# A fused attention, Fourier-mix and MLP kernel: loads in a new order, and batch 1 by the way of the later batches

## The chip, the cores and the metric

The kernel runs on one core of one Trainium2 chip. The metric is device time of one execution in microseconds, the median of several runs. The engines are TensorE (PE; its weight loads are listed as PEld), VectorE (DVE), ScalarE (ACT), GpSimd (POOL) and SyncE (SP, which here only issues DMAs).

## The reference, cut to what matters

Two layers in a row, over 4 batches of 768 positions, 8 heads of 64 (512 features).

```python
# attention: q, k, v are (4, 8, 768, 64)
scores = q @ k.T / 8
keep   = (pos_k < 8) | ((0 <= pos_q - pos_k) & (pos_q - pos_k < 96))
dist   = where(pos_k < 8 and not local, 96, abs(pos_q - pos_k))
scores = where(keep, scores - slope[h] * dist, -1e9)
x      = softmax(scores) @ v            # heads side by side: (4, 768, 512)

# Fourier mix and MLP
u   = x + real(fft(fft(x, axis=positions), axis=features))
un  = (u - mean(u)) / sqrt(var(u) + 1e-6)
out = u + relu(un @ w_ch1) @ w_ch2      # w_ch1 (512, 2048), w_ch2 (2048, 512)
```

## The kernel before, in words

**The order of the work.** The program is written out by a planner (class `Plan`, lines 18 to 153) that runs once, when the kernel is built. It keeps a clock for every engine and for the DMA queues, with a cost for each step. Four lists of TensorE work wait in it: `MIX` (Fourier and normalisation), `ATT` (attention), `PH` and `PG` (the two MLP products). At each step it emits what can start first by its clocks; between equals an earlier list goes first. Work of the other engines, and each DMA issue, is queued with `pl.later` and goes to the engine that would end it first. What comes out is a fixed order on each engine; a semaphore wait stands wherever data or a buffer must be ready. SP and POOL issue their DMAs in that fixed order too, and a wait on one of them holds all that is behind it.

**Attention of one batch.** Heads go in four pairs. `load` brings q, k and v of a pair (384 KB each); `cast_qk` or `cast_direct` turns q and k to 16 bits; `trans` transposes them (twelve 128x128 products on PE and a copy `qkT` by DVE, L515 and L521, or, for batches 2 and 3, four DMA transposes, `trans_dma`, L494); `kg_copies` takes the 8 global keys out on POOL. `score` makes a pair's banded scores in three units. `glob`, `v_global` handle the global keys. `av` multiplies by v and its `norm` (L699, L700) writes the batch's x. Two ways exist:

- Batches 0 and 1: v is cast by POOL (`cast_v0`) and put in place by PE (`v_place`, L427, copies L443 and L444). The bias is added on PE by products of a diagonal `sid` with the distances `dist` (L542, L547), and ACT's exponential (L575) writes `ex` directly.
- Batches 2 and 3: v comes by a strided DMA (L336) and is cast in place (`cast_v`, L454). The exponential goes to `er` (L572) and DVE multiplies it by a table `mk` (L587). ACT makes `mk` with eight exponentials (L1128).

**Fourier mix of one batch.** `bounce` writes x to DRAM (`xd`) and reads it back with rows in another order (`xr`), on ACT's queue. `fold_3` (batch 0) or `fold_s` and `fold_d` add and subtract on DVE; `y_unit` (py, L881) is the transform over positions with tables `t1` and, in batch 0, `t1x`; `mirror` makes reversed copies on POOL (L916 to L918, L929); `u_unit` (pu, L961) is the transform over features, and its `add` (L980, L984) makes u and its mean; `un`, `nt_unit` (ptu, L1025) normalise and transpose.

**MLP.** A chunk is 256 rows; there are three in a batch. `ph_unit` (ph, L1053) makes 8 units of 8 products for a chunk, `pg_unit` (pg, L1076) 8 units of 4, and L1085 adds the result to u, which L1090 stores. Three chunks of `hT` fit.

**Loads and PSUM.** SP issues batch 0's loads, then batch 1's; q and k of batch 1 are staged in the buffers that later hold w1 and w2. POOL issues w1 and w2 (four parts each, fp32 in DRAM, cast by the DMA) when the casts of batch 1 have left those buffers (`wload`, L1164, L1169). SP then waits for the last part of w2 (`hold`, L1178) before the loads of batch 2. Four PSUM banks serve attention of batches 0 and 1 as rings `C` and `D`; when the last of these uses is over (token `("CD",)`) they become the banks of ph and pg.

```python
1180:         for b in range(B):
1181:             if b:
1182:                 for hp in range(HP):
1183:                     load(b, hp, "qk")
1184:                     load(b, hp, "v")
```

Of the kernel before, what the change touches and what calls it, by code (L numbers as in the profile page):

```python
# [14 lines left out]
P = 128  # L15


class Plan:
# [10 lines left out]
    def __init__(self):  # L29
        self.t = {"PE": 0.0, "ACT": 0.0, "DVE": 0.0, "POOL": 0.0, "SP": 0.7, "DMA": 1.9, "DMA2": 0.0}  # L30
        self.tok = {}
        self.ready = []
        self.pending = []
        self.rings = {}
        self.left = {}
        self.n = 0
# [49 lines left out]
    def emit(self, place):  # L86
# [6 lines left out]
        if dma:  # L93
            q = "DMA2" if eng == "ACT" or outs and outs[0][0] in ("xw", "xr") else "DMA"
            end = self.t[q] = max(self.t[q], end) + dma
        else:
            lat += self.LAT.get(eng, 0.0)
# [79 lines left out]
def kernel(  # L177
# [23 lines left out]
    FB = 2  # L201
    DB = 1
    assert (B, H, S, Dh, NG, NL) == (4, 8, 768, 64, 8, 96)
# [66 lines left out]
    def bank(tag, name, dtype=FP32):  # L270
# [4 lines left out]
        if "late" not in early:  # L275
# [6 lines left out]
            "ww": 1, "rev0": 1, "u": 4, "un": 2, "unT": 2, "w1": 1, "w2": 1}  # L282
# [21 lines left out]
    one = kon.tile([P, 1], FP16, tag="one", name="one")  # L304
    expst = [kon.tile([P, 2, 1408], FP16, tag=f"ex{hp}", name=f"ex{hp}") for hp in range(HP)]
# [13 lines left out]

    def load(b, hp, which):  # L320
        n = HP * b + hp
        h0 = 2 * hp
        gate = [("gate",)] if n == FB * HP else []
        if b >= FB:
            srcs = [(0, q), (1, k)] if which == "qk" else [(2, v)]
            for w, src in srcs:
                i = 2 + 3 * (n - FB * HP) + w

                def run(src=src, i=i, w=w):
                    t = stage[("t", n, w)] = buf("qs", i, [P, 2 * NS, Dh], FP32, 1)  # L330
# [6 lines left out]
                pl.later([("SP", 0.55 if w < 2 else 1.1, run)], free("qs", i) + gate, 0.0, [("ld", n, w)], lat=1.7, dma=2.67)  # L337
                if w < 2:
                    cast_direct(b, hp, w, i)
# [5 lines left out]
        else:  # L345
            tag, ti, users, slot = (("hT", hp, 2, 0) if hp < 3 else ("qs", 0, 1, None)) if b == 0 else \
                (("w1", "w2")[hp // 2], 0, 4, 2 * (hp % 2))
            for w, src in enumerate((q, k)):
                at = (tag, ti) if slot is not None else (tag, w)

                def run(w=w, src=src, at=at):
                    if slot is None:
                        t = buf(at[0], at[1], [P, NS, 2 * Dh], FP32, 1)
                    else:
                        if at not in stage:
                            stage[at] = buf(at[0], at[1], [P, users, NS, 2 * Dh], FP32, users)
                        t = stage[at][:, slot + w]
                    stage[("t", n, w)] = t
                    run_dma(t, src, b, h0)
# [15 lines left out]
    def cast_qk(b, hp, w, at):  # L375
# [9 lines left out]
        if b == 0 and not (w and hp):  # L385
            ways.append(("DVE", dve2(768), lambda: cast("DVE")))
        elif b == 0:
            ways = [("POOL", 0.87, lambda: cast("POOL"))]
        else:
            ways.append(("POOL", 0.87, lambda: cast("POOL")))  # L390
        pl.later(ways, [("ld", n, w)] + free("qk", n), 0.0, [("qk", n, w)], [("free",) + at], rank=b)

    def cast_direct(b, hp, w, i):
        n = HP * b + hp

        def cast(on):
            if n not in qk16:
                qk16[n] = buf("qk", n, [P, 2, 2, NP, 2, Dh], FP16, 1)
            for t in range(2):
                copy_on(on, qk16[n][:, t, w], stage[("t", n, w)].rearrange("p (h i t) d -> p t i h d", h=2, t=2)[:, t])  # L400
        pl.later([("ACT", act(768), lambda: cast("ACT")), ("POOL", 1.6, lambda: cast("POOL"))],
                 [("ld", n, w)] + free("qk", n), 0.0, [("qk", n, w)], [("free", "qs", i)], rank=1)
# [46 lines left out]
    def cast_v(b, hp):  # L449
        n = HP * b + hp  # L450
        i = 2 + 3 * (n - FB * HP) + 2
# [4 lines left out]
        pl.later([("POOL", 0.87, run)], [("ld", n, 2), ("avdone", b - 2)], 0.0, [("v", b, hp)], [("free", "qs", i)], rank=1)  # L456
# [6 lines left out]
    def BANKS(b):  # L463
        return ("xx", "C", "D") if b < 2 else ("xx",)

    def CD(b, ring):
        if b == 1 and ring in ("C", "D"):
            pl.left[("CD",)][0] += 1
            return [("CD",)]
# [4 lines left out]


# [27 lines left out]
    def trans(b, hp):  # L503
        if b >= FB:
# [3 lines left out]
        def run(start, ring):  # L508
            pt = bank("xx", f"pt_{n}", FP16)
            src = qk16.pop(n)  # L510
            for w in range(2):
                o = pt[:, w, 0:S].rearrange("p (n a t m) -> p n t a m", n=NP, a=2, t=2)
                for x in range(NP):
                    for t in range(2):
                        nc.tensor.transpose(o[:, x, t], src[:, w, x, t].rearrange("p h d -> p (h d)"), idn)  # L515
# [3 lines left out]
            def evac():  # L519
                TT[n] = buf("qkT", n, [P, 2, S], FP16, 6)  # L520
                V.tensor_copy(TT[n], pt[:, :, 0:S])  # L521

            def evac_act():
                TT[n] = buf("qkT", n, [P, 2, S], FP16, 6)
                A(TT[n], pt[:, :, 0:S], AF.Copy)
            pl.later([("DVE", dve2(2 * S), evac)] + [("ACT", act(2 * S), evac_act)] * (b < 2), free("qkT", n), e, [("qkT", n)], ring=ring, rank=RA(b))
            kg_copies(b, hp)
        ATT.append(([("qk", n, 0), ("qk", n, 1)], ("xx",), run))

    def score(b, hp, g):  # L530
        n = HP * b + hp
        idx = 2 * HP + 3 * (n - 2 * HP) + g

        def run(start, ring):
            pa = bank(ring, f"sc_{n}_{g}")
            w0, w1_ = ((256, CO), (CO, CO), (256, P))[g]
            tiles = ((2 * g, 0, w0), (2 * g + 1, 256, w1_))
            if b < 2:
# [10 lines left out]
            for i, c0, cw in tiles:  # L549
                for s in range(2):  # L550
                    lo = 64 * s
                    nc.tensor.matmul(pa[:, s, c0:c0 + cw], TT[n][lo:lo + 64, 1, i * P:(i + 1) * P],  # L552
                                     TT[n][lo:lo + 64, 0, i * P:i * P + cw], start=(b > 1), stop=True,
                                     skip_group_check=(b < 2))
            e = pl.pe(0.24 if b > 1 else 0.66, start)
# [17 lines left out]
            if b < 2:  # L573
                def direct():
                    A(cut(expst[hp][:, :, g * 512:g * 512 + (384 if g == 2 else 512)]), cut(pa), AF.Exp, 0.0, 0.125)  # L575
                pl.later([("ACT", act(2 * w), direct)], [("avh", 0, hp)] * b, e, [("ex", b, hp, g)], CD(b, ring), ring=ring, rank=RA(b))
# [3 lines left out]
            def mul():  # L580
# [4 lines left out]
                else:  # L585
# [3 lines left out]
                     [("er", idx), ("mk", hp)] + ([("avh", b - 1, hp)] if b else []), 0.0,  # L589
                     [("ex", b, hp, g)], [("free", "er", idx)], rank=RA(b))  # L590
        ATT.append(([("qkT", n)] + ([("sid", hp), ("c", "dist")] if b < 2 else []), BANKS(b), run))
# [58 lines left out]
    XT = [("x", 0), ("hT", 4), ("x", 1), ("x", 2)]  # L650
# [58 lines left out]
    def bounce(b):  # L709

        on, eng = "ACT", nc.scalar
# [16 lines left out]
        pl.later([(on, 0.5, rd)], [("xw", b, n) for n in range(len(parts))] + free("xr", b), 0.0, [("xr", b)], lat=1.7, dma=3.8 if b else 2.4)  # L728
# [53 lines left out]
    def IW(b, n):  # L782

        return 2 * b + n if b < DB else 3 * b - DB + n

    def fold_3(b):
# [17 lines left out]
        def g1():  # L804
            z = T[("z", b)]
            eg = T[("eg", b)] = buf("eA", IA(b, 0), [P, 2, 6, 256], FP16, 1)
            ww = T[("ww", b)] = buf("ww", IW(b, 0), [P, 20, P], FP16, 1)
# [20 lines left out]
    T1X = {}  # L828

    def fold_d(b, needs):  # L830
# [3 lines left out]
        def g1():  # L834
            z = T[("z", b)][:, 0:6]
            eg = T[("eg", b)] = buf("eA", ia, [P, 2, 6, 256], FP16, 1)
            ww = T[("ww", b)] = buf("ww", IW(b, NA(b)), [P, 20, P], FP16, 1)
# [29 lines left out]
    def y_unit(b, g):  # L867
        def run(start, ring):
# [17 lines left out]
            if g == len(YG) - 1:  # L886
                pl.used(("free", "eA", IA(b, NA(b))), e)
                pl.used(("free", "ww", IW(b, NA(b))), e)
            nb = (len(ys) + 1) // 2

            def cp(on, lo, hi):
                if ("y", b) not in T:
                    T[("y", b)] = buf("zy", 2 * b + 1, [P, 8, 2, 2, P], FP16, 7)
# [5 lines left out]
                for t in range(lo, hi):  # L899
                    for a in range(2):  # L900
                        Y[(b,) + ys[2 * t + a]] = T[("y", b)][:, 2 * g + t, a]
            cuts = [(0, nb)] if b else [(t, t + 1) for t in range(nb)]
            for x, (lo, hi) in enumerate(cuts):
                w = 512 * (hi - lo)
                pl.later([("ACT", act(w), lambda lo=lo, hi=hi: cp("ACT", lo, hi)),
                          ("DVE", dve(w), lambda lo=lo, hi=hi: cp("DVE", lo, hi))],
                         free("zy", 2 * b + 1), e, [("y", b) + y for y in ys[2 * lo:2 * hi]],
                         (CD(b, ring) if x == len(cuts) - 1 else []), ring=ring if x == len(cuts) - 1 else None)
        MIX.append(([("w", b, 0 if g in (0, 3) else 1)] + [("c", "t1")] + [("c", "t1x")] * (b < DB), BANKS(b), run))

    def mirror(b):

        def r0():
# [375 lines left out]
```

## Time and profile before

| | |
|---|---|
| median of 3 runs | 278.57 us (278.4 to 279.12) |
| profiled execution | 280.46 us, of which the span of the trace is 278.7 |
| granted TensorE clock | 0.999 |
| busy, share of span | PE 93%, PEld 62%, DVE 57%, ACT 53%, POOL 22% |
| PE products | 2448, in 258.7 us |
| HBM read, written | 31.92 MB, 9.44 MB |
| chain that ended last | PE 81%, DVE 8%, ACT 4% |

In the page, the busy tenths are the span in 40 slices of about 7 us. A row of the timeline is start, length, engine, source line, operation, output and inputs, and how many instructions were merged into it; lengths of products overlap, so a rate is read from the starts. "us to landing" of a DMA is from issue to the last byte.

### The profile page before, as it was taken

What the parts mean: (1) busy time and instruction counts of PE and PEld (TensorE: products, weight loads), DVE (VectorE), ACT (ScalarE), POOL (GpSimd) and SP (SyncE); (2) the same over time, 40 slices, a digit from 0 to 9 for tenths busy, and PEclk for the clock granted to TensorE, in tenths of its full rate; (3) what the DMA queues carried; (4) which work ended last, traced back from release to release, by engine and by line L of the source; (5) the groups of instructions that cost most, each with busy time, mean ns of one, the idle gap of its engine ahead of it and who ended that gap; (6) DMA issues with size and microseconds to landing.
All of it is one profiled execution on the core that took longest, in us unless ns stands there. A gap on an engine that the chain in (4) does not pass through costs nothing.

```text
span 278.7 us, 6005 instructions
## 1 busy us (share of the span) xinstructions
PE 258.7 (93%) x2448; PEld 173.2 (62%) x2448; DVE 157.9 (57%) x323; ACT 148.0 (53%) x255; POOL 60.8 (22%) x127
## 2 busy tenths in 40 slices
PE   1999789598789999999999999999999999999994
PEld 1445538458657874677486466777866677767441
DVE  4347781985786414766278968666896661111121
ACT  1466675495666642797782237889242256434000
POOL 1435365931002512412110021401001320100000
PEclk9999999999999999999999999999999999999999
DMA  7999999997774498978858895200164020110122
GB/s 206 290 291 257 339 304 196 207 204 119 194 204 144 105 167 162 231 137 165 196 146 196 214 263 104 66 2 0 40 136 168 1 78 1 40 38 22 56 75 75
DMA packets 70301, 40.69 MB, mean 146 GB/s; under 512 B 27394, under 2 KB 66306, under 8 KB 70274
## 3 DMA queue, kind: packets, MB, share of 16 engines
q1 hardware_dynamic: 61474, 29.83, 43.6%
q0 software_dynamic: 4224, 4.19, 9.3%
q10 hardware_dynamic: 4576, 6.29, 8.3%
q8 instruction: 19, 0.31, 0.5%
q14 instruction: 8, 0.07, 0.1%
HBM read 31.92 MB, written 9.44 MB: 148 GB/s over the span
## 4 chain that ended last, share of the span: by engine, by line
PE 81%; DVE 8%; ACT 4%; issue 2%; DMA 2%; POOL 1%; ACTq 1%; SPq 0%; DVEq 0%; POOLq 0%
PE pg L1076 29%; PE ph L1053 29%; PE py L881 5%; PE sc L552 4%; PE pav L680 3%; PE pu L961 3%; ACT ex L575 2%; PE pt L515 2%; DVE qkT L521 2%; PE ptu L1025 2%; DMA ident<-idm 2%; PE sc L547 2%; PE pav L669 1%; PE sc L542 1%; DVE sm L984 1%
## 5 line engine op out<-in xcount | busy, mean ns | idle before, releaser
L1053 PE MATMUL ph<-unT,w 128*128 128x256 f16 x768 | 93.8, 273 | 2.2 <-DVE hT L1060 2.2
L1076 PE MATMUL pg<-w,hT 128*128 128x512 f16 x384 | 89.9, 379 | 0.0
L1053 PEld LDWEIGHTS <-w 128*128 128x128 f16 x768 | 72.7, 98 | 18.4 <-issue 6.1
L1059 ACT ACTIVATE hT<-ph 128x512 f16<-128x512 f32 x73 | 43.6, 597 | 48.1 <-PE ph L1053 46.9
L1076 PEld LDWEIGHTS <-hT 128*128 128x128 f16 x384 | 36.8, 98 | 36.3 <-issue 0.4
L1085 DVE SCALAR_TENSOR_TENSOR u<-pg,sm,u 128x512 f32<-128x512 f32 x24 | 18.0, 750 | 53.7 <-PE pg L1076 53.5
L575 ACT ACTIVATE ex<-sc 128x992 f16<-128x992 f32 (+2 forms) x24 | 21.3, 925 | 15.1 <-PE sc L552 11.1
L1060 DVE TENSOR_SCALAR hT<-ph 128x512 f16<-128x512 f32 x23 | 15.9, 690 | 11.5 <-PE ph L1053 11.5
L572 ACT ACTIVATE er<-sc 128x992 f16<-128x992 f32 (+2 forms) x24 | 21.5, 923 | 1.6 <-PE sc L552 1.6
L1011 POOL TENSOR_SCALAR sm<-sm 128x2 f32<-128x2 f32 x12 | 3.2, 264 | 71.9 <-ACT un L1004 71.7
L929 POOL COPY ww<-zy 128x512 f16<-128x512 f16 x16 | 9.4, 613 | 42.4 <-PE py L881 42.4
L980 DVE SCALAR_TENSOR_TENSOR u<-pu,xr 128x512 f32<-128x512 f32 x24 | 15.6, 688 | 4.7 <-PE pu L961 4.0
L552 PE MATMUL sc<-qkT 64*128 64x256 f16 (+1 forms) x192 | 17.8, 275 | 0.2 <-DVE qkT L521 0.2
L369 ACT ACTIVATE qk<-qs 128x384 f16<-128x384 f32 (+1 forms) x31 | 14.5, 528 | 6.1 <-DMA qkT<-qk 4.8
L587 DVE TENSOR_TENSOR ex<-er,mk 128x992 f16<-128x992 f16 (+2 forms) x24 | 15.2, 645 | 3.8 <-ACT er L572 3.6
L995 ACT ACTIVATE un<-u,sm 128x512 f16<-128x512 f32 x12 | 8.5, 716 | 16.1 <-DVE sm L984 13.0
L680 PE MATMUL pav<-v,ex 128*128 128x65 f16 x352 | 16.4, 193 | 0.4 <-ACT ex L575 0.4
L680 PEld LDWEIGHTS <-ex 128*128 128x128 f16 x352 | 15.1, 97 | 1.8 <-issue 1.1
L552 PEld LDWEIGHTS <-qkT 64*128 64x128 f16 x192 | 6.0, 96 | 16.1 <-issue 13.2
L896 ACT ACTIVATE zy<-py 128x512 f16<-128x512 f32 (+1 forms) x10 | 8.1, 810 | 14.7 <-PE py L881 14.7
L1004 ACT ACTIVATE un<-un 128x512 f16<-128x512 f16 x24 | 14.8, 620 | 1.5 <-PE ptu L1025 1.4
L898 DVE CAST zy<-py 128x512 f16<-128x512 f32 (+1 forms) x9 | 8.3, 927 | 10.5 <-ACT zy L896 6.4
(101 smaller groups left out, 305.8 us busy)
## 6 DMA issues: line engine op xcount, KB each, us to landing
out_dram<-u SPq DMA_DIRECT2D x24, 256.0 KB, 2.2
w<-in_moe_w_ch_dram POOLq DMA_DIRECT2D x8, 512.0 KB, 11.8
qs<-in_q_dram SPq DMA_DIRECT2D x9, 384.0 KB, 4.7
qs<-in_k_dram SPq DMA_DIRECT2D x9, 384.0 KB, 5.4
u<-in_v_dram SPq DMA_DIRECT2D x8, 384.0 KB, 7.7
xr<-xd ACTq DMA_DIRECT2D x4, 768.0 KB, 4.3
qs<-in_v_dram SPq DMA_DIRECT2D x16, 192.0 KB, 3.9
w<-in_q_dram SPq DMA_DIRECT2D x4, 384.0 KB, 7.5
```

Source lines behind the costliest of these rows:

```text
L552: nc.tensor.matmul(pa[:, s, c0:c0 + cw], TT[n][lo:lo + 64, 1, i * P:(i + 1) * P], TT[n][lo:lo + 64, 0, i * P:i * P + cw], start=(b > 1), s ...
L572: A(mine(), cut(pa), AF.Exp, 0.0, 0.125)
L575: A(cut(expst[hp][:, :, g * 512:g * 512 + (384 if g == 2 else 512)]), cut(pa), AF.Exp, 0.0, 0.125)
L587: VT(o, mine(), m, op=ALU.mult)
L680: nc.tensor.matmul(po[:, jj, hh * 65:(hh + 1) * 65], lhsT, v16[b % 2][:, i, h, 0:65], start=(jp == 0 and a == 0), stop=(a == len(ops) - 1) ...
L980: V.scalar_tensor_tensor(u[:, a].rearrange("p (n r) -> p n r", r=4), pu[:, a].rearrange("p (r n) -> p n r", r=4), 1.0, XR[b][:, rr].rearra ...
L1004: A(x, x, AF.Square, accum_out=MV[c][:, a, 2:3])
L1053: nc.tensor.matmul(ph[:, a * CH:(a + 1) * CH], W1[0][:, d, jb * P:(jb + 1) * P], UNT[c][:, d, :], start=(d == 0), stop=(d == ND - 1))
L1059: pl.later([("ACT", act(512), lambda: A(dst, ph, AF.Relu)), ("DVE", dve(512), lambda: V.tensor_scalar_max(dst, ph, 0.0))], [], e, [("h", c ...
L1060: ("DVE", dve(512), lambda: V.tensor_scalar_max(dst, ph, 0.0))],
L1076: nc.tensor.matmul(pg, HT[c][:, jb, t * P:(t + 1) * P], W2[0][:, jb, :], start=(jb == 0), stop=(jb == NJ - 1))
L1085: V.scalar_tensor_tensor(UT[c][:, t, :], pg, MV[c][:, t, 3:4], UT[c][:, t, :], op0=ALU.mult, op1=ALU.add)
```

## The change

- **Batch 1** goes by the way of the later batches (`FB` from 2 to 1): v by the strided DMA, no `v_place`, no bias products, `er` and the product with `mk`. Its q and k are still transposed on PE (`PT`). `mk` is therefore made at the start (`MKA`). Only batch 0 uses the rings `C` and `D`.
- **Loads.** After batch 0: the tables `t1`, `t2`, q and k of pairs 0 and 1 of batch 1 (`EARLY`, into w2's buffer), `t1x`. w1 has a buffer free from the start and is issued when batch 0's last k is cast (`W1AT`). Batch 0's bounce is issued by SP. w2 is held by a two-element POOL copy (`seen`) until the bounce's read has landed. The rest of batch 1 is issued after that read (token `("xi",)`) into the three `qs` buffers. Batch 2 waits for part 2 of w2 (`WG`). The planner's costs of these DMAs are lowered.
- **Products of zeros.** Twelve 512-column products of the zeroed tile `EG` stand first on PE.
- **Small copies.** The global keys of a pair transposed on PE are copied from PSUM by the engine that copies `qkT` (`kg_now`). The reversed copies of `mirror`'s first part, and all of batch 0's, are made from PSUM by ACT or DVE (`back`, `turn`); batch 0's go to space behind `t1x`. In batch 0 ACT makes the mean instead of DVE.

```diff
-    FB = 2
+    FB = 1
     DB = 1
+    WG = 2
+    MKA = 4
+    EARLY = [(4, 0), (4, 1), (5, 0), (5, 1)]
+    W1AT = ("qk", 3, 1)
+    PT = (0, 1, 2, 3)
...
+    order = [(n, w) for n in range(HP, B * HP) for w in range(3) if n >= HP + 2 or w == 2]
+    def place(n, w):
+        return ("qs", 2 + order.index((n, w))) if (n, w) in order else ("w2", 0)
...
-                pl.later([("SP", 0.55 if w < 2 else 1.1, run)], free("qs", i) + gate, 0.0, [("ld", n, w)], lat=1.7, dma=2.67)
+                pl.later([("SP", 0.55 if w < 2 else 1.1, run)], free(*at) + gate + [("xi",)] * (b == 1 and (n, w) not in EARLY), 0.0, [("ld", n, w)], lat=1.7, dma=1.47 if w < 2 else 2.3)
...
     def BANKS(b):
-        return ("xx", "C", "D") if b < 2 else ("xx",)
+        return ("xx", "C", "D") if b == 0 else ("xx",)
...
+    def kg_now(b, hp, on, pt):
+        for s in range(2):
+            c0 = 16 * (hp % 2) + 8 * s
+            d = kG[b % 2][64 * s:64 * s + 64, hp, c0:c0 + NG].rearrange("p (t m) -> p t m", t=2)
+            x = pt[64 * s:64 * s + 64, 1, 0:P].rearrange("p (t m) -> p t m", t=2)[:, :, 0:NG // 2]
+            copy_on(on, d, x)
...
-            if b < 2:
+            if b == 0:
                 for s in range(2):
                     lhsT = sid[:, 2 * hp + s, :]
...
-        on, eng = "ACT", nc.scalar
+        on, eng = ("ACT", nc.scalar) if b else ("SP", nc.sync)
...
+            def back(on):
+                d = T[("y", b)][:, 7]
+                s0 = py[:, 0, :].rearrange("p (a c m) -> p a c m", a=2, c=2)
+                copy_on(on, d[:, 0, :, 0:1], s0[:, 0, :, 0:1])
+                copy_on(on, d[:, 0, :, 1:P], s0[:, 0, :, P - 1:0:-1])
+                copy_on(on, d[:, 1], s0[:, 1, :, ::-1])
+            def turn(on, t):
+                d = REV[0][:, 2 * g + t]
+                copy_on(on, d.rearrange("p a c m -> p (a c) m"), py[:, t, :].rearrange("p (x m) -> p x m", m=P)[:, :, ::-1])
...
-                V.tensor_scalar_mul(sm[:, :, 1], sm[:, :, 0], -SC / Dm)
+                if b:
+                    V.tensor_scalar_mul(sm[:, :, 1], sm[:, :, 0], -SC / Dm)
+                else:
+                    A(sm[:, :, 1], sm[:, :, 0], AF.Copy, 0.0, -SC / Dm)
...
+        V.memset(EG, 0.0)
+        pz = bank("xx", "pz")
+        for _ in range(12):
+            nc.tensor.matmul(pz[:, 0, :], EG[:, 0:P], EG, start=True, stop=True)
...
+                    nc.gpsimd.tensor_copy(seen, XR[0][0:1, 0, 0:2])
                     W2[0] = buf("w2", 1, [P, NJ, Dm], FP16, 1)
...
-            needs = [("vc", 5), ("free", "w1", 0)] if i == 0 else [("wl", 3), ("free", "w2", 0)] if i == 4 else [("wl", i - 1)]
+            needs = [W1AT] if i == 0 else [("wl", 3), ("free", "w2", 0), ("xr", 0)] if i == 4 else [("wl", i - 1)]
...
-            nc.sync.dma_start(g, W2[0][0:1, NJ - 1, 0:2])
-        pl.later([("SP", 0.45, hold)], [("w2", 3)], 0.0, [("gate",)])
+            nc.sync.dma_start(g, W2[0][0:1, 4 * WG, 0:2])
+        pl.later([("SP", 0.45, hold)], [("w2", WG)], 0.0, [("gate",)])
```

## The prediction

> **What bounds the kernel now.** I read the page's busy row first, then busy time by window, then the chain of waits in order of time, then the timeline around the places the chain names.
>
> ```profile
> PE 258.7 (93%) x2448; PEld 173.2 (62%) x2448; DVE 157.9 (57%) x323; ACT 148.0 (53%) x255; POOL 60.8 (22%) x127
> ...
> PE   1999789598789999999999999999999999999994
> ```
>
> TensorE is the bound, and all that it loses it loses early. Busy time by window says how much (columns: length, then PE busy and its instructions, and the other engines):
>
> ```profile
> 6.20:64.30 58.10, 50.91 (x633) 30.04 (x634) 38.30 (x87) 37.56 (x57) 30.20 (x51) 1.00 1.13 260
> 64.30:100.00 35.70, 33.08 (x339) 26.89 (x336) 21.12 (x40) 22.00 (x41) 6.33 (x11) 1.00 0.62 152
> 100.00:274.80 174.80, 174.67 (x1484) 116.29 (x1481) 95.47 (x186) 87.16 (x157) 23.26 (x56) 1.00 0.45 107
> ```
>
> From 100 us on PE never stops. Before 64.3 us DMA is full (share 1.13), while DVE and ACT are busy 66% and 65%. The timeline shows more loss inside "busy":
>
> ```profile
> 6.39 1.46 PE L515 MATMUL pt<-ident,qk 128*128 128x128 f16 x12
> 19.49 0.84 PE L515 MATMUL pt<-ident,qk 128*128 128x128 f16 x12
> 37.61 0.58 PE L547 MATMUL sc<-dist,sid 128*128 128x496 f16 x2
> 38.12 0.39 PE L552 MATMUL sc<-qkT 64*128 64x256 f16 x4
> 38.44 0.58 PE L542 MATMUL sc<-dist,sid 128*128 128x480 f16 x2
> 134.77 0.59 PE L552 MATMUL sc<-qkT 64*128 64x256 f16 x8
> 135.29 1.90 PE L1076 MATMUL pg<-w,hT 128*128 128x512 f16 x8
> ```
>
> The same twelve transposes take 1.46 us at 6.4 and 0.84 at 19.5. A score unit with bias products takes 0.83 us (37.61 to 38.44), two without take 0.52 (134.77 to 135.29). And the chain gives the milestones of batch 0:
>
> ```profile
> 42.16 6.66 PE py L881 x60
> 48.82 0.91 PE pu L961 x16
> ...
> 51.16 2.78 DVE sm L984
> ...
> 64.50 0.87 PE ph L1053 x8
> ```
>
> The channel mix (ph, pg) starts only at 64.3 us: its weights are still landing (w2 until 69.5), its PSUM banks are shared with batch 1's attention, and the third pu waits for POOL's mirrors until 60.3.
>
> **Sum of the old early stage.** Work at full rate before 64.3, from warm rows. Batch 0: 4 transposes x 0.84 = 3.4, 12 score units x 0.78 (mean of 0.83, 0.82, 0.69) = 9.4, v placement 4 x 0.23 (24 in 0.46) = 0.9, global tokens 2 x 0.55 = 1.1, av 4.0 (0.46 + 0.7 + 0.8 for pairs 0 and 1, 2.0 for 2 and 3), py 6.7, pu 3 x 0.91 = 2.7, two ptu 0.9: 29.1. Batch 1, in the same order but only as far as it has come by then: 3.4 + 9.4 + 0.9 + 0.8 + 1.6 = 16.1. Together 45.2, in 64.3 - 6.2 = 58.1 us: 12.9 us lost, about 4.5 of it the slow rate before 19.5, the rest waits.
>
> **The change, part by part.**
>
> *PE work removed.* Batch 1 has no bias products: 12 units x (0.78 - 0.27) = 6.1 us; no v placement: 0.9. Both lie on the engine that sets the end: -7.0 us.
>
> *Products of zeros.* 12 of 512 columns. The 496-column bias pair stood 0.94 us apart early (14.92 to 15.86), so 0.47 each: 5.7 us, from 1.2 (DVE's memset of EG, 0.27 us, moved first) to about 7. PE waits there for ident until 6.17, so they cost between 0 and 0.8 us. What they bring: the transposes drop by 0.6 each and the score pairs by 1.6 (3.98 against 2.34), up to 4.5 us. PEclk is printed as 1.00 throughout, so only these durations show the rate. I count this inside the milestone below, not again. The Trainium skill (TensorE: Matmul & The Clock Gate, The HAM clock gate) says that about 3.4 us of sustained activity doubles the rate and one idle window of that length halves it again; our trace needed 13 us from its first product, so the rule would make this gain certain and the trace leaves it open.
>
> *Load order.* Batch 0's last v lands at 21.6 (issue 13.93 + 7.7). Behind it on SP now stand t1, t2, q and k of two pairs of batch 1 and t1x: 1.27 MB + 1.57 MB, at the 290 GB/s of this stage 9.8 us, so 31.4 with nothing beside them. POOL starts w1 at about 21: 205 GB/s (4.19 MB in 20.4 us) makes 10.2 us for half. t1x, which the first py needs, thus lands between 31.4 and 41.6; I take 37.5, the middle rounded up. Batch 0's bounce moves from ACT's queue to SP's, behind these loads: write, write, read. Its read landed at about 46 (issue 41.61 + 4.3); now between 40 and 50, I take 45. What SP holds behind that wait is the rest of batch 1, which is told to wait anyway. The Trainium skill (DMA: Bandwidth & Descriptors, Queues, rings and completion order) says each DMA engine takes turns between queues packet by packet; that speaks against early w1, and by it t1x would come at the late end and the sum would be some 3 us smaller.
>
> *Batch 0's chain.* The last k is there at 19.0 (12.34 + 6.7) but POOL cast it at 21.89, behind kG copies that waited for DVE. Those leave POOL. Cast at 20, then transpose, scores, av as before (21.9 to 34.95) puts the last norm at about 32, with the quick clock 31. ACT gets mk here (8 x 0.73 = 5.8 us, from 74 to 81 before); it idles 6.4 us up to 9.54, which covers it; uncovered it costs up to 3 us of exps. From last norm to py took 7.1 us, of which two qkT copies 1.9: py at 31 + 5 = 36 or with t1x, 38. pu at 38 + 6.7 = 44.7, with the read at 45. Then three DVE adds of 1.4 to 1.5 without the 2.78 us stall of sm (it goes to ACT) and without POOL's mirrors (ACT or DVE turn from PSUM, 4 x 0.69 + 1.0 more): the third ends at about 50.5. Only batch 0 holds the ph banks now. So ph starts at **51**, bounds 46 (t1x early) to 57 (t1x at 41.6, read at 50).
>
> *New waits.* On POOL a two-element copy (`seen`) reads the bounce's result before w2 is issued, so POOL stands until about 45. Behind it are four w2 issues (0.79 each) and batch 1's later casts, whose loads are not there before 45 either: nothing is held that could run, save casts of the early q and k, which ACT can take. SP's hold of batch 2 now follows w2's third part, not its last: at 205 GB/s 2.55 us earlier. Cost of both on the path: 0; if a cast of pair 1 stood behind `seen`, its two transposes and six units (3.3 us of PE) would go from before 51 to after it, which is up to 3.3 us more lost.
>
> *DVE and ACT.* Batch 1 gains 12 products with mk (0.645 each, 7.7), 16 kG copies (about 0.16, the 32x4 cast: 2.6), turns and backs 6.8, and loses 4.5 of v copies: +12.6 us on two engines that had 40 us free in 6 to 64. Hidden; if that cover were gone, some 3 us.
>
> *New early sum.* Until 51 PE can do batch 0's 29.1 and of batch 1 two transposes (1.7) and six units (1.6): 32.4. Lost: 51 - 6.2 - 32.4 = 12.4 against 12.9. In general the change is (start of ph) - 58.5: at 51, **-7.5 us**. The profiled execution (280.46, span 278.7, 1.8 around it) lies 1.9 above the median 278.57; from the median: **271.0 us**; 266 for 46, 277 for 57. After that ph of three chunks waits for no w2, and the 2.6 us lost in 64 to 100 I keep (0 to 5).
>
> **What may be late next.** Counting pg products by window: 76 of 96 were done by 113.5, and by 175.5 these:
>
> ```profile
> 113.50:175.50 62.00, 26.00 (x112) 10.52 (x112) 1.00 0.81 179
> ```
>
> 188 of 192: four products (0.9 us) were left to cover for batch 2's chain. If PE comes earlier, batches 1 and 2 must come earlier too. Batch 2's loads began at 69.9, after w2; now at about 65.
>
> **The rivals.**
>
> *Slower: batch 1 comes late.* Its other 8 loads wait for the bounce's read and share DMA with w2 and three buffers that POOL must free. From 51 PE has ph and pg of three chunks (24 x 0.87 + 24 x 0.86 = 41.5), batch 1's rest (7.8) and its py, pu, ptu (6.2): until 106.5. From batch 1's last norm (72.4) its unT could be there 24.5 us later (97), so the norm is needed by 82. Forecast: 41 + 2.4 + 10.2 + 10.9 (3.15 MB) = 65, plus batch 0's 13.4 from last load to last norm: 78.5, 3.5 us to spare. From 89.5 on the kernel is slower than before; at 94, 283 us. For it: SP waited 4.4 us for POOL's v cast. Chance 0.18.
>
> *No change: t1x, xr and w1 crowd each other* and ph starts at 57 to 59.5: 278. For it: DMA full until 65. Chance 0.12.
>
> *Much faster:* the zeros take 4.5 us out of batch 0's chain, ph starts at 46, and the 2.6 us of 64 to 100 go too: 264. Chance 0.18.
>
> *Forecast:* 0.52, its own range 266 to 276.
>
> Measurement tells about 0.3% (0.8 us) from no change. Faster: 0.52 + 0.18 + 0.05 of the second rival = 0.75; same 0.05; slower 0.18 + 0.02 = 0.20. The range reaches from 263 to 280: it leaves out most of the slow rival and the far end of the fast one.
>
> **What would show it.** Right: first transposes at 0.84; py near 38; first ph near 51; PE in the first 60 us about as idle as now, with 24 fewer bias products; no wait of PE after 100. Wrong: a PE wait between 95 and 115 or near 165 (batch 1 or 2 late); py waiting for the DMA of t1x past 42; transposes at 1.46; ph waiting for its evacuation by DVE or ACT between 51 and 75.

## The result and the profile after

The changed kernel takes **297.25 us**, the median of 4 runs (296.73 to 301.71), against 278.69 for the kernel before beside it (4 runs, 278.4 to 279.12): ratio 1.0659, 95% interval 1.0634 to 1.0683. The run of 301.71 fell in a slower state of the chip, and the ratio is that of the other runs. The profiled execution took 297.47, its span is 295.7 and the granted clock 0.951, where before had 0.999. The page of the changed kernel, the rows on TensorE:

```profile
PE 263.2 (89%) x2388; PEld 174.4 (59%) x2388; DVE 168.3 (57%) x354; ACT 149.5 (51%) x271; POOL 48.3 (16%) x93
...
PE   7599369659999859989999699999999999999993
...
PEclk9989877958999998999999999999999999999999
```

There are 60 products fewer than before, as the change says, and PE is busy 4.5 us longer (263.2 against 258.7). Its idle time, span less busy, went from 20.0 to 32.5 us. Both together are the 17.0 us between the spans. The third row is new: before, the clock was printed as 9 in all slices; here it drops in the slices where PE also drops, and right behind them. Busy time by window, cut at the first ph and at the end of batch 1's py (columns as in the prediction; last three: clock, DMA share, GB/s):

```profile
6.05:64.92 58.87, 41.28 (x470) 26.12 (x465) 35.90 (x92) 36.79 (x63) 13.78 (x18) 0.83 1.14 241
64.92:113.50 48.58, 44.30 (x420) 31.82 (x419) 31.95 (x59) 30.09 (x60) 11.30 (x19) 0.92 0.93 194
113.50:291.80 178.30, 173.19 (x1489) 114.88 (x1487) 98.12 (x193) 81.29 (x149) 22.21 (x47) 1.00 0.37 88
```

Up to the first ph PE idles 17.6 us (58.87 less 41.28) where it idled 7.2. After it 4.3 and 5.1 us more, where before lost 2.75 in all. What PE waits for, longest first, and what ACT waits for of loads (columns: in total, times, longest):

```profile
PE sc L567 <- ACT er L587: 3.7, 4, 1.5
PE pav L684 <- ACT eg L660: 3.2, 1, 3.2
PE py L897 <- ACT zy L911: 3.1, 1, 3.1
PE pt L529 <- ACT ex L590: 3.0, 1, 3.0
PE pt L529 <- ACT qk L382: 3.0, 1, 3.0
```

```profile
ACT qk L382 <- DMA qs<-in_q_dram: 8.5, 4, 4.4
...
ACT qk L382 <- DMA qs<-in_k_dram: 5.4, 2, 2.8
...
ACT qk L382 <- DMA w<-in_k_dram: 3.3, 1, 3.3
```

All five name ACT, yet ACT is busy only 51%: it stands still itself, 17.2 us in all (the sum of the three rows), in casts whose data have not landed, while other work is queued behind. (The largest sum among all of ACT's waits, 66.1 us, is for ph and stands in another row.) Three places in the timelines show how it goes. First, batch 0's start (PE, then ACT):

```profile
1.18 4.18 PE L1147 MATMUL pz<-eg 128*128 128x512 f16 x12 [1.18 <-DVE eg L1144]
6.05 0.84 PE L529 MATMUL pt<-ident,qk 128*128 128x128 f16 x12
13.17 0.83 PE L529 MATMUL pt<-ident,qk 128*128 128x128 f16 x12 [3.02 <-ACT ex L590]
14.23 0.95 PE L562 MATMUL sc<-dist,sid 128*128 128x496 f16 x2
```

```profile
6.82 3.87 ACT L1162 ACTIVATE mk<-dist 128x640 f16<-128x640 f16 x6 [4.81 <-DMA dist<-distm]
10.59 2.53 ACT L590 ACTIVATE ex<-sc 128x992 f16<-128x992 f32 x3
```

The zeros did what they were forecast to do: the transposes take 0.84 us at 6.05. But mk can start only when its table `dist` has landed, at 6.82, and its six exponentials then hold the first `ex`; PE waits 3.02 us, and the products of the bias go back to 0.95 us a pair (0.58 at 6.84). Second, the global tokens of batch 0:

```profile
33.88 0.94 ACT L382 ACTIVATE qk<-w 128x384 f16<-128x384 f32 x2 [3.33 <-DMA w<-in_k_dram]
34.84 0.68 ACT L660 ACTIVATE eg<-pgl,gb 32x512 f16<-32x512 f32 x1
```

```profile
35.57 0.29 PE L684 MATMUL pav<-vG,eg 128*128 128x130 f16 x1 [3.23 <-ACT eg L660]
```

`eg` is all that batch 0's av lacks, and it stands behind the cast of batch 1's second k, issued at 20.34 and landed 13.5 us later. Third, the same again at the first ph, with a k of pair 2 and `un`:

```profile
62.49 0.94 ACT L382 ACTIVATE qk<-qs 128x384 f16<-128x384 f32 x2 [2.84 <-DMA qs<-in_k_dram]
63.33 0.70 ACT L1024 ACTIVATE un<-u,sm 128x512 f16<-128x512 f32 x1
```

```profile
63.07 1.13 PE L529 MATMUL pt<-ident,qk 128*128 128x128 f16 x6 [2.99 <-ACT qk L382]
64.09 1.04 PE L1054 MATMUL ptu<-ident,un 128*128 128x128 f16 x8
64.92 3.62 PE L1082 MATMUL ph<-unT,w 128*128 128x256 f16 x16
...
72.74 1.91 PE L1082 MATMUL ph<-unT,w 128*128 128x256 f16 x16
```

The first 16 ph products take 3.62 us, sixteen later ones 1.91: half the rate, for the time after a wait. Around 110 us the scene repeats with batch 2's q (ACT waits 4.42 until 109.10; PE's py waits 3.06 until 110.57).

### The profile page after: what moved, and what is told of

Read it like the earlier page. It is cut to its first block, busy times and chain, and to the rows that moved or that the text cites. A ratio compares the mean times of both kernels' runs of the same rounds, so it can differ in the third digit from the quotient of the medians.

```text
span 295.7 us, 5906 instructions
## 1 busy us (share of the span) xinstructions
PE 263.2 (89%) x2388; PEld 174.4 (59%) x2388; DVE 168.3 (57%) x354; ACT 149.5 (51%) x271; POOL 48.3 (16%) x93
## 3 DMA queue, kind: packets, MB, share of 16 engines
q0 software_dynamic: 4224, 4.19, 8.5%
## 5 line engine op out<-in xcount | busy, mean ns | idle before, releaser
L1088 ACT ACTIVATE hT<-ph 128x512 f16<-128x512 f32 x70 | 41.7, 595 | 66.6 <-PE ph L1082 66.1
L587 ACT ACTIVATE er<-sc 128x992 f16<-128x992 f32 (+2 forms) x36 | 33.0, 918 | 9.9 <-PE sc L567 6.6
L602 DVE TENSOR_TENSOR ex<-er,mk 128x992 f16<-128x992 f16 (+2 forms) x36 | 22.5, 626 | 14.5 <-ACT er L587 14.4
L1089 DVE TENSOR_SCALAR hT<-ph 128x512 f16<-128x512 f32 x26 | 18.0, 691 | 14.1 <-PE ph L1082 14.1
L382 ACT ACTIVATE qk<-qs 128x384 f16<-128x384 f32 x36 | 16.7, 513 | 16.0 <-DMA qs<-in_q_dram 8.5
L715 DVE TENSOR_TENSOR x<-pav,rc 128x512 f16<-128x512 f32 (+1 forms) x27 | 17.1, 632 | 0.9
L464 POOL CAST v<-qs 128x768 f16<-128x768 f32 x12 | 10.5, 873 | 39.4 <-DMA qs<-in_v_dram 28.4
L897 PE MATMUL py<-t,ww 128*128 128x256 f16 x76 | 13.1, 295 | 3.0 <-ACT er L587 1.8
L529 PE MATMUL pt<-ident,qk 128*128 128x128 f16 x96 | 7.7, 230 | 7.8 <-ACT ex L590 3.0
L384 DVE COPY qkT<-pt 128x1536 f16<-128x1536 f16 x8 | 7.7, 957 | 10.9 <-PE pt L529 10.9
```

The costliest lines, as they stand in the source:

```text
L382: A(d, s, AF.Copy)
L587: A(mine(), cut(pa), AF.Exp, 0.0, 0.125)
L602: VT(o, mine(), m, op=ALU.mult)
L715: VT(X[b][:, 2 * jp:2 * jp + 2, first * Dh:(first + nh) * Dh].rearrange("p j (h d) -> p j h d", d=Dh), pv[:, :, :, 0:Dh], rc.to_broadcast( ...
L897: nc.tensor.matmul(o, lhsT, rhs, start=(x == 0), stop=(x == len(ops) - 1))
L1088: pl.later([("ACT", act(512), lambda: A(dst, ph, AF.Relu)), ("DVE", dve(512), lambda: V.tensor_scalar_max(dst, ph, 0.0))], [], e, [("h", c ...
```

## The experiments

**The theories.** *Order:* the planner now believes that loads are cheap and that weights do not slow them (new clock `DMAW`, 1.47 and 2.3 in place of 2.67). It puts casts of batch 1 and 2 on ACT ahead of work that is ready, and the fixed order keeps them there. *One wait:* a single misplaced step (mk, or the early k) costs its wait and the slow rate behind it. *Bytes:* w1 and w2 share the DMA engines with the loads, and any order would suffer. *Work:* what DVE and ACT got from PE is the loss. A caution for all: an edit that the planner sees (a cost, a token, a list) rewrites the whole order; only `a_fill`, `a_w_quarter`, `b_w_quarter` and `b_zeros` keep it.

**1. The planner's costs alone, on the kernel before** (`b_new_costs`).

```diff
-            q = "DMA2" if eng == "ACT" or ...
+            q = "DMAW" if eng == "POOL" else "DMA2" if eng == "ACT" or ...
-    lat=1.7, dma=2.67)
+    lat=1.7, dma=1.47 if w < 2 else 2.3)
```

> The kernel before with only the planner's costs of the change (1.47 and 2.3 us a load, 2.6 a weight part on a clock of its own). No transfer and no arithmetic changes, only the order in which instructions are written out. Theory 'order': ACT's casts move ahead of their data in batches 2 and 3, PE gets waits after 100 us: 281 to 287. Rival 'contention': 278 to 279.5, as before.

Measured 281.61, ratio 1.0104 (1.0052 to 1.0157). The costs alone make it slower, though only by 2.9 us. The time is in the range of the order theory, but the late casts that it named are not there: PE idles 3.4 us between 100 and 276 us, in waits for `u` and hT, and ACT's casts wait 1.9 us for loads in all.

**2. The costs alone, undone in the change** (`a_costs_back`: the inverse of that diff, and 3.3 again for the weights in place of 2.6).

> The changed kernel with the planner's old costs for loads and weights (2.67 and 3.3 us each, one shared DMA clock): the same transfers and the same arithmetic, another order of instructions. Theory 'order' (ACT's casts of q and k stand too early in its order, wait there for a DMA, and hold exponentials and copies that PE needs): ACT's waits for loads, 17.2 us in the changed kernel (8.5 for q, 5.4 for k, 3.3 for the early k), fall below 6, PE's waits fall with them, time 280 to 288. Rival 'contention' (w1, tables and early loads crowd the DMA engines and everything is late for that): the transfers are the same, so 294 to 298.

Measured 288.1, 1.0337 (1.0212 to 1.0462): 9 us of the 18.6 come back. py starts at 38.14 and ph at 54.42, and ACT waits 2.1 us for loads in place of 17.2. The rest of the loss has another face, since now batch 1 is placed too late. SP issues no load from 64.9 to 79.2, because a store of `u`, whose data come at 78.7, stands ahead of it; DVE is busy 0.75 us of the ten from 70 to 80; and PE waits until 110.76 for DVE's sums:

```profile
PE py L897 <- DVE ww L856: 4.2, 1, 4.2
```

**3. One clock** (`a_one_clock`: the new costs, but weights and loads on one planner clock) **and costs in between** (`a_oc_mid_mk`: one clock, 2.0 and 2.5, and all of mk after batch 0).

```diff
-            q = "DMAW" if eng == "POOL" else "DMA2" if eng == "ACT" or ...
+            q = "DMA2" if eng == "ACT" or ...
```

> The changed kernel with the change's own costs (1.47, 2.3, 2.6 us) but weights and loads on one DMA clock in the planner. Theory 'order': the plan is then neither too early for the loads beside the weights nor too late for batch 1; ACT's waits for loads fall below 6 us and PE has no wait near 105 as with the old costs (4.2 us); 278 to 285. Rival 'contention': 288 or more, as with the old costs, since the transfers are the same.

> The same kernel with the planner's load costs between the old and the new (2.0 and 2.5 instead of 1.47 and 2.3; the old were 2.67). If the remaining loss is a matter of costs that are closer to what the loads take: 279 to 283. If any order that the planner writes meets one late cast or another: 283 to 289, with the waits of PE in other places.

Measured 291.59, 1.0436 (1.0274 to 1.0598), and 287.45, 1.0271 (1.0226 to 1.0316). The first is above the 288 that was to speak for bytes; in it batch 0 is as late as ever (py 42.89), so the gain lies later. The second has py at 35.26 and ph at 56.32, and is still 8 us slower than before, in the second of its two ranges.

**4. One wait after the other** (`a_mk_late`, `a_fill`, `a_early`, `a_early_hold`, `a_pool_casts`).

```diff
-    MKA = 4
+    MKA = 0                       # a_mk_late
+            if b == 0 and part == (2,) and jp == 1:      # a_fill: 8 products of
+                for _ in range(8):                       # 512 columns before eg's wait
+                    nc.tensor.matmul(po[:, 0, :], idn, dist_sb[:, 0:512], ...)
-    dma=1.47 if w < 2 else 2.3
+    dma=2.9 if (n, w) in EARLY else 1.47 if w < 2 else 2.3   # a_early
+                    nc.gpsimd.tensor_copy(seen, stage[("t", 5, 1)][0:1, 0, 0:2])   # a_early_hold: a_early, w1 after this k
-    [("ACT", act(768), lambda: cast("ACT")), ("POOL", 1.6, lambda: cast("POOL"))]
+    [("POOL", 1.6, lambda: cast("POOL"))]                # a_pool_casts
```

> The changed kernel with the eight exponentials of mk made after batch 0's last scores instead of at the start. Theory 'mk first on ACT delays the first exponentials': PE's wait of 3.0 us before the second pair's transposes (at 10 to 13) goes, the granted clock stays full from 10 to 20, time 291 to 294. Theory 'order': that wait goes too, but batch 0 is held again by ACT's wait for the early k that lands at 33.9, so 295 to 297.

> The changed kernel, same order, with eight extra 512-column products put on PE just before the product that waits 3.2 us for eg (at 32 to 35.6 us); their result is overwritten. Theory 'clock' (a PE wait of about 3 us halves the rate of the products behind it): the granted clock stays at 1.0 in 40 to 50 us, py's 60 products take 6.7 us instead of 9.7, 2 to 4 us less in all: 293 to 295. Rival 'the rate is lost for another reason': 297 to 299.

> The changed kernel with one planner cost other: 2.9 us instead of 1.47 for the four early loads (q and k of two pairs of batch 1), so that the plan has them at about 34 us, where they landed. Theory 'order': ACT casts the last of them after eg instead of before it, batch 0's last norm comes at 33 instead of 39, py at 38, the first ph at 55 to 57; alone it takes 4 to 7 us off: 290 to 293. Rival 'contention': the loads are as late as before, batch 1 is late by it, 295 to 298.

> As a_early, but POOL reads the last early k before it issues w1, so w1 starts when that load has landed (about 29 to 31 us) instead of at 20.4. Theory 'contention': early k lands at 29 to 31 instead of 33.9, t1x with it, batch 0's py a few us earlier, 2 to 5 us below a_early. Theory 'order': what is gained there is lost on the bounce, which now shares the DMA engines with w1: within 2 us of a_early or slower.

> The changed kernel with the casts of q and k of batches 1 to 3 on POOL alone, planner's costs as changed. Theory 'order': ACT waits for no load any more (17.2 us before), PE's waits behind ACT (eg 3.2, zy 3.1, qk 3.0, un 1.8, er 5.5) shrink by more than half, time 280 to 288. Rival 'contention': POOL waits in ACT's place, the data come no earlier, 293 to 298.

Measured 298.03 (ratio 1.0693), 298.14 (1.0718), 299.8 (1.0777), 296.4 (1.0655) and 294.9 (1.0581, interval 1.0526 to 1.0637): four of the five gain nothing, and the interval of the fifth still touches that of the change (1.0634 to 1.0683). In each the wait that was aimed at went or shrank. `a_mk_late` has the full clock from 10 to 20 and ph at 56.45, and then loses more:

```profile
PE sc L567 <- ACT er L587: 7.4, 4, 3.9
PE pu L992 <- ACT zy L382: 4.9, 1, 4.9
PE pt L529 <- ACT qk L382: 4.6, 4, 3.0
```

`a_fill` kept the clock at 1.00 from 30 to 40 (0.83 in the change), the av products took 0.22 and 0.28, and py was at half rate all the same after three more waits of about 1 us. `a_early` has py at 39.12, 3.7 us earlier, and ph no earlier than 64.35, because the next casts stand where these stood (ACT, then PE's wait):

```profile
60.66 0.94 ACT L382 ACTIVATE qk<-qs 128x384 f16<-128x384 f32 x2 [5.79 <-DMA qs<-in_k_dram]
61.51 0.70 ACT L1024 ACTIVATE un<-u,sm 128x512 f16<-128x512 f32 x1
```

```profile
PE ptu L1054 <- ACT un L1024: 5.0, 1, 5.0
```

In `a_early_hold` the two early casts wait no more (30.55, right behind `eg`), and PE then waits 4.6, 4.5 and 4.2 us in ptu and py. `a_pool_casts` moves the waits to POOL: PE's pt waits 7.4 us for its casts. The theory of one wait falls: no single one of these waits is worth the loss.

**5. The weights' bytes, the order kept** (`a_w_quarter`, `b_w_quarter`).

```diff
-    nc.gpsimd.dma_start(W1[0][:, :, a * 512:(a + 1) * 512], moe_w_ch1[:, a * 512:(a + 1) * 512]...)
+    nc.gpsimd.dma_start(W1[0][:, 0:1, a * 512:(a + 1) * 512], moe_w_ch1[0:P, a * 512:(a + 1) * 512]...)
...
-    nc.gpsimd.dma_start(W2[0][:, 4 * a:4 * a + 4, :], moe_w_ch2[a * 512:(a + 1) * 512, :]...)
+    nc.gpsimd.dma_start(W2[0][:, 4 * a:4 * a + 1, :], moe_w_ch2[a * 512:a * 512 + P, :]...)
```

> The change with each of the eight weight transfers cut to its first 128 rows of 512 (a quarter of the bytes; the products read those rows again, so the output is another, with as many products as before). No instruction moves. If the waits come from loads that share the DMA engines with w1 and w2: the early k of pair 1 lands by 27 instead of 33.9, no wait of PE before the global tokens, last norm about 35, first ph about 55, total 282 to 288. If the order itself loses the time, whatever the loads do: first ph after 62, total 293 to 297.

> The kernel before with the same cut of the weights' bytes, as the other half of the comparison. Its own order was calm about the loads: 275 to 279. If it gains as much as the changed kernel does, sharing with the weights is not what tells the two apart.

Measured 289.55, 1.0359 (1.0316 to 1.0402), and 277.87, 0.9958 (0.9935 to 0.998). With the same instructions in the same order the change gets about 8 us back, the kernel before 1.2. The wait of `eg` is gone; the k is cast 3 us earlier:

```profile
30.83 0.94 ACT L382 ACTIVATE qk<-w 128x384 f16<-128x384 f32 x2 [0.35 <-DMA w<-in_k_dram]
```

It landed 10.6 us after its issue, not by 27 as I expected: the other loads, t1x among them, fill the engines too (the DMA share is full from 20 to 24 us here as well). 10.5 us of the loss stay with a quarter of the bytes; ACT still waits 8.4 us for q of later pairs. So bytes are a part. The kernel before is a weak counterpart: there POOL issues the weights from 42.67 on, when SP has issued the last load of batch 1 (by 37.0), so the loads hardly share with them. That its order would stand the same sharing is not shown.

**6. Several edits at once** (`a_oc_w1`: one clock, `W1AT` at the cast of the early k; `a_oc_mk`: one clock, mk late; `a_oc_early_mk`: that and 2.9 for the early loads; `a_oc_mk_noxi`: `a_oc_mk` without the `("xi",)` token).

```diff
-    W1AT = ("qk", 3, 1)
+    W1AT = ("qk", 5, 1)                                      # a_oc_w1
-    free(*at) + gate + [("xi",)] * (b == 1 and (n, w) not in EARLY)
+    free(*at) + gate                                         # a_oc_mk_noxi
```

> As a_one_clock, but w1 is issued only after the early k of batch 1's second pair is cast (order on POOL), some 8 to 12 us later. Theory 'contention': early q, k and t1x land 5 us or more earlier, batch 0's last norm is at 32 instead of 38 to 39 as in the changed kernel, py starts near 36; 3 to 6 us below a_one_clock. Theory 'order': the plan already allows for w1, so within 2 us of a_one_clock, or later because ph then waits for w1.

> As a_one_clock, with mk after batch 0's last scores. Theory 'order': with the early k no longer in the way the wait of 2.6 to 3.0 us at 10 to 13 matters little, within 1.5 us of a_one_clock. Theory 'clock' (every PE wait of about 3 us halves the rate of what follows): the wait at 10 to 13 goes and with it the half rate until 17, 2 to 4 us below a_one_clock.

> The three edits together that theory 'order' asks for: one DMA clock, 2.9 us for the early loads, mk after batch 0's last scores. The wait at 10 to 13, the one for eg and ACT's early waits for loads go; first ph at 53 to 56; 276 to 281, at least 3 us below a_oc_mk (284.7). Rival 'contention': 283 to 286.

> The change with one planner clock for weights and loads and all of mk later (284.7 when run alone), and in addition the rest of batch 1 no longer told to wait for the bounce. If that hold is what makes batch 1 late: batch 1's first py before 95 instead of 98.3, no PE wait in 100 to 110, 278 to 281. If not: 284 to 288, since the loads then share with the bounce.

Measured 284.12 (1.0168), 284.67 (1.0188), 284.86 (1.024) and 292.95 (1.0458). The first three meet at 284 by different roads, all slower than before (the intervals start at 1.0013, 1.004 and 1.0145). `a_oc_w1` does not work as meant: w1 starts at 22.2 instead of 20.5, the early k still lands at 33.66 and py starts at 42.66; what it gained lies later, in another order, with PE busy 29.2 of the 30 us from 100 to 130. Without the hold behind the bounce the loads of batch 1 push out the table that batch 0 needs:

```profile
PE py L897 <- DMA hT<-t1xm: 8.6, 1, 8.6
```

t1x is issued there at 28.12 instead of 23.15. So dropping the hold costs more than it gives; a shorter hold, until t1x has landed, was not tried.

**7. Two parts of the change alone** (`b_zeros`: the twelve products put into the kernel before; `b_nobias`: batch 1's masks by mk in the kernel before; `a_bias`: batch 1's bias products put back into the change).

```diff
+        V.memset(EG, 0.0)                                     # b_zeros
+        for _ in range(12):
+            nc.tensor.matmul(pz[:, 0, :], EG[:, 0:P], EG, start=True, stop=True)
-            if b < 2:                                         # b_nobias (a_bias: the inverse)
+            if b == 0:
...
-            pl.later([("ACT", 2 * act(NM), m)], [("c", "dist"), ("x", 1, 3, 2)], ...)
+            pl.later([("ACT", 2 * act(NM), m)], [("c", "dist"), ("ex", 0, 3, 2)], ...)
```

> The kernel before with only the twelve products of zeros at first. Theory 'clock': the first transposes take 0.84 us instead of 1.46, the exponentials of pair 0 start 1 us or more earlier; batch 0's chain then meets its loads (last k at 19.0), so 276.5 to 278.5. Rival 'they only delay' (the rate does not rise by zeros, first transposes stay at 1.46): 278.5 to 279.5.

> The kernel before with one part of the change alone: batch 1's masks are multiplied in from mk (with two buffers of its own for the exps, and mk made after batch 0's exps), so that its 12 score units lose their bias products. If PE work taken away is worth its time where nothing else moves: 6 us less, 271 to 274. If PE only waits longer for DVE and ACT, which get the 12 multiplications and an earlier mk: 277 to 283.

> The change with that one part undone: batch 1's scores get their bias products back and its exps go straight to the rows, without mk. If the part is worth 6 us inside the change too: 301 to 304. If the change's waits swallow what PE has less to do: 294 to 299, with as much idle time of PE less as it gets more to do.

`b_zeros`: 278.34, ratio 0.9951 (0.9921 to 0.9982), the only kernel here with the full computation that beats the one before, in the same order. It is a small gain: the medians of the kernel before itself lie between 277.99 and 279.88 from one session to the next. `b_nobias`: 279.75, 1.0028 (0.9999 to 1.0057). `a_bias`: 298.23, 1.066 (1.0613 to 1.0708), where the change has 1.0659. What was exchanged, bias products on PE for mk on ACT and its product on DVE, is worth nothing either way. The pages show where the time went, `b_nobias` first, then `a_bias`:

```profile
PE 256.5 (92%) x2424; PEld 174.3 (63%) x2424; DVE 164.0 (59%) x335; ACT 148.5 (54%) x255; POOL 61.7 (22%) x127
...
PEclk9999977979999999999999999999999999999999
```

```profile
PE 267.6 (90%) x2412; PEld 177.4 (60%) x2412; DVE 159.0 (54%) x340; ACT 152.8 (52%) x277; POOL 44.0 (15%) x89
```

In `b_nobias` PE's busy time falls by 2.2 us, not 6.1, and the clock drops in three slices between 35 and 62, which fits; a new wait of 2.6 us stands before py, for the exponential `es` of batch 1 that is to be multiplied. In `a_bias` PE is busy 4.4 us longer and idle 3.5 us less. PE had less to do, and waited for what came next.

**All of them by one measure.** Spans, milestones and PE's page row; idle is span less busy:

| kernel | first ph | batch 1's last norm | py of batch 2 | span | busy | idle |
|---|---|---|---|---|---|---|
| before | 64.3 | 72.4 | 159.9 | 278.7 | 258.7 | 20.0 |
| the change | 64.9 | 91.6 | 169.8 | 295.7 | 263.2 | 32.5 |
| b_zeros | 62.0 | 70.1 | 157.6 | 276.3 | 259.7 | 16.6 |
| a_mk_late | 56.5 | 92.8 | 169.3 | 297.2 | 264.6 | 32.6 |
| a_costs_back | 54.4 | 102.5 | 170.4 | 286.4 | 261.6 | 24.8 |
| a_w_quarter | 58.4 | 84.9 | 162.1 | 287.9 | 260.7 | 27.2 |
| a_oc_w1 | 60.2 | 94.3 | 163.1 | 282.8 | 261.6 | 21.2 |
| a_oc_mk | 57.1 | 89.1 | 157.9 | 282.4 | 258.2 | 24.2 |

The first ph says nothing about the end. `a_costs_back` has it 10 us earlier than before, and ends 8 us later. What sets the two families apart is batch 1: its last norm ends between 69.8 and 78.3 us in the kernel before and its variants, and between 84.9 and 102.5 in the change and all of its variants. No experiment brought it back, and among the variants it does not order the times either.

**Against what was expected.** Neither theory held its numbers throughout. `a_costs_back` came out at the edge of the range for order. `a_pool_casts`, `a_one_clock`, `a_early_hold` and `a_oc_early_mk` came out at the numbers for contention, and `a_fill` at those of its rival. `a_w_quarter` fell between its two ranges; `a_mk_late`, `a_early`, `a_oc_w1`, `a_oc_mk` and `a_oc_mk_noxi` fell outside both of theirs. Order (9 us) and bytes (about 8 us) each carry about half of the loss when undone alone; the two were not undone together. In part 7 `b_zeros` came out as the theory of the clock said, and `b_nobias` and `a_bias` as the theory said that waits swallow the work.

## Why the prediction was wrong

**The formula failed first.** The prediction made the time from one milestone: "the change is (start of ph) - 58.5". With the measured 64.92 it gives +6.4 us; the spans differ by 17.0. `a_mk_late` would be 2 us faster by it and is 18.5 slower. The formula takes for granted that PE runs on once ph starts. It can hold only while there is other work to cover batches 1 and 2, and the prediction had the number at hand (188 of 192 products done, 0.9 us of slack). By 113.5 us the changed kernel had done 192 ph products (before 195) and 40 pg products (before 76): 36 products of 0.216 us, 7.8 us behind. Of the 10.6 us that the formula misses, idle time is 6.6 (9.4 less 2.75) and the rest, about 4, fits the lower clock (0.92 over the 48.6 us from the first ph).

**Start of ph: 51 predicted, 64.92 measured.** The 13.9 us are three steps. py started at 42.86 instead of 38 (4.9). It took 9.8 us instead of 6.7 to pu (3.1), up to 48.3 at half rate. From pu to ph went 12.3 instead of 6.3 (6.0), with the waits at 57.5 and 63.07. The last norm, for which 31 was forecast, ended at 39.04; from there to py less time went than forecast.

**The term that was wrong in kind: "Cost of both on the path: 0", "which ACT can take".** The prediction looked at what stands behind the new waits of POOL and SP. It did not look at what stands behind the casts on ACT. There `eg`, `un` and zy stood behind casts whose data had not landed, and `ex` behind mk. ACT's free time was counted as cover ("40 us free in 6 to 64"), but a free engine that waits inside its fixed order covers nothing. mk was said to be covered by the 6.4 us that ACT idled up to 9.54, "uncovered it costs up to 3 us"; `dist` landed only at 6.82, so most of that idle time could not be used, and it cost 3.02 of PE. "Planner's costs are lowered" stands in the description of the change, and no step of the prediction gave it a price; undone alone it is worth 9 us, the largest single part that was found.

**PE work: -7.0 predicted.** The products did go. In exchange for mk they were worth nothing in time, alone or inside the change (1.0028 and 1.066): PE waited for what came next.

**Zeros: right, and forgotten in the sum of risks.** 4.18 us for 5.7 forecast, transposes at 0.84, and alone 0.9951. Even there the milestone says too much: py starts 3.2 us earlier in `b_zeros` than before (38.88 for 42.09), the first ph 2.3, and the time falls by 1.4. In the change the clock was then taken as won. After each of its four waits of 2.99 to 3.23 us the products went back to half rate for a few microseconds, so these waits cost more than their length. PE's busy time exceeds the forecast by 7.3 us (258.7 - 7.0 + 4.2 = 255.9 against 263.2), and the lower clock (0.951 in the mean) is the only thing I found in the trace that lengthens its products.

**Load order.** t1x was not late in the change, and the bounce's read was seen at 48.25 for 45 forecast, inside its range. The weights were priced too low: 205 GB/s came from "4.19 MB in 20.4 us", but in the kernel before they are issued from 42.67 on and have landed at 69.5, 26.9 us later. In the change w1, for which 10.2 us were counted, has parts that land up to 17.9 us after their issue.

Of the rivals, "batch 1 comes late" named the right mechanism: batch 1's last norm ended at 91.56, past the 89.5 from which it was to decide. The forecast had batch 1's last load in by 65. These rows (SP, ACT, POOL) show why it was late:

```profile
53.44 3.28 SPq L354 DMA_DIRECT2D qs<-in_v_dram  x2
58.89 2.60 SPq L378 DMA_DIRECT2D qs<-in_q_dram  x1
63.45 0.81 SPq L378 DMA_DIRECT2D qs<-in_k_dram  x1
69.93 1.30 SPq L354 DMA_DIRECT2D qs<-in_v_dram  x2
```

```profile
57.95 0.92 ACT L382 ACTIVATE qk<-qs 128x384 f16<-128x384 f32 x2
68.97 0.94 ACT L382 ACTIVATE qk<-qs 128x384 f16<-128x384 f32 x2 [0.89 <-DMA qs<-in_q_dram]
```

```profile
74.94 0.82 POOL L464 CAST v<-qs 128x768 f16<-128x768 f32 x1 [1.16 <-DMA qs<-in_v_dram]
```

These loads share three `qs` buffers, and SP issues the last three each at the moment a cast ends: q of pair 3 at 58.89, after ACT's cast of pair 2's q (until 58.87; its data were there 5.6 us after the issue at 47.91, but the cast stood behind `un`); k at 63.45, after the cast that waited until 62.49; v at 69.93, after the cast of 68.97. So the last load landed just before 74.94, not by 65. The rival's price was far too low: its scale (even at 89.5, 283 us at 94) gives some 281 us for 91.56, and 297.25 was measured. It counted one late chain, no other wait beside it and no drop of the clock.

**What stays open.** Costs, bytes and combinations bring the change to 284, 4 to 7 us over the kernel before on the same chip. Whether an order exists that makes the whole change faster was not found; no single cause was shown for these last microseconds. All variants of the change share batch 1's late last norm; a fourth `qs` buffer, or loads of batch 1 held until t1x instead of the bounce's read, would test it, and neither was run. In `a_oc_early_mk` PE's largest waits are spread over `er`, zy, kG and qkT, none over 2.8 us in total.

## What to carry to other kernels

When the order is written by a planner, its costs are part of the change: price what each engine's queue would do if a load came 5 us later than the planner thinks, above all on the engine that both casts loads and feeds the bound engine. A milestone is a forecast only if the work behind it is shown to be there; compare products done by a given time, not the start of a stage. Busy time taken off the bound engine is no gain where the next input is late, and the quickest test is to put that part alone into the kernel before.

## What the runs showed of the hardware

A wait has a price beyond its length, and not always. The kernel before and `b_zeros` have the same wait of 2.50 us before the same products (PE, before first):

```profile
54.75 0.62 PE L1025 MATMUL ptu<-ident,un 128*128 128x128 f16 x8 [2.50 <-ACT un L995]
55.21 0.83 PE L515 MATMUL pt<-ident,qk 128*128 128x128 f16 x12
```

```profile
51.54 0.62 PE L1025 MATMUL ptu<-ident,un 128*128 128x128 f16 x8 [2.50 <-ACT un L995]
52.00 1.25 PE L515 MATMUL pt<-ident,qk 128*128 128x128 f16 x12
```

In the first the rate stayed. In the second it fell to half (granted clock 0.57 from 52 to 56, 1.00 from 56 on). The Trainium skill (TensorE: Matmul & The Clock Gate, The HAM clock gate) says that the clock is lowered after an idle window of about 3.4 us, and that the windows run freely rather than from the kernel's start. A free-running window would fit that the same wait counted in one kernel and not in the other. But a wait shorter than 3.4 us was enough here, and so were the 3.02 and 2.99 us of the change.

A 384 KB load of q or k landed 4.7 (q) and 5.2 us (k; medians) after its issue from 120 us on, and the early k took 13.5 us beside four weight transfers of 512 KB. With those cut to a quarter it took 10.6.
